# Weight conversion without a clamp and half of its low parts on TensorE, V laid out with zeros, two small copies on ScalarE, one attention layout for all units

## The chip, the cores and the metric

The kernel runs on one core of a Trainium2 chip. The time is device time in microseconds (us) of one execution, and the number compared is the median over several executions. The engines are named as the profile names them: PE (TensorE, the matrix engine; PEld is its weight load), DVE (VectorE), ACT (ScalarE), POOL (GpSimd), SP (SyncE, which here only issues DMAs).

## What is computed

A gated linear attention, a dense layer with a three-way maximum, and a mixture of experts with two of eight experts for each token. All arrays are float32, and the weights of the dense layer reach the chip as 64-bit floats, so that the kernel itself has to make 32-bit numbers of them.

```python
for t in range(S):                                  # B=4, H=8, S=768, D=48
    state = alpha[:, :, t, :, None] * state + np.einsum('bhd,bhe->bhde', k[:, :, t], v[:, :, t])
    y[:, :, t] = np.einsum('bhd,bhde->bhe', q[:, :, t], state)
x = y.transpose(0, 2, 1, 3).reshape(3072, 384)
h = np.maximum(np.maximum(x @ w1, x @ w2), x @ w3)  # 384 -> 768
x = h @ w_out                                       # 768 -> 384
noisy = x @ w_gate + np.log1p(np.exp(x @ w_noise)) * noise
# the two largest of eight, their softmax, then for each chosen expert e:
out[mask] += weight * (np.maximum(x[mask] @ w1[e], 0) @ w2[e])
```

## The kernel before

**Precision by two parts.** The large products are made of fp32r numbers in a high part (`hi`, a cast) and a low part (`lo`, the value minus `hi`), three matmuls for one (`THREE`). So every operand is split on its way: by ACT (the cast) and by DVE or POOL (the subtraction).

**Weights.** Twelve pieces of 128 x 768 64-bit numbers come by DMA into `RAWH`, `RAW` and `RAWO`: nine for the dense layer (`wconv(0)` to `wconv(8)`) and three for the output projection. `dissect` (L200) makes one piece into fp32 with integer operations on the two 32-bit words, in a tile `cb` of which there are two: ACT takes the absolute value of the high word (L206), POOL clamps it from below (L207), DVE shifts it (L208) and puts in the sign and the low bits (L209, L210), ACT casts the high part out (L212) and POOL subtracts to get the low part (L213). A piece can start when one of the two `cb` tiles is free again.

**Attention.** 24 units of 128 rows (two half batches of channels side by side on the partitions), each of four heads' chunks: `prep_a` makes the running product of alpha (`D`, L279) and its reverse (`kh`, L282, and POOL's product with k at L283), and copies eight columns twice on DVE (into `Z` at L277, into `en` at L285). `prep_x` multiplies q (`X1`, `X2`). `prep_v` copies V from the loaded tile `vn` into `vbd`, which holds zeros where one head meets the other (L315); `prep_l` copies V into `l` (L307). On PE: `att_t` transposes `kh`, `att_s` makes the scores, `att_g` the states, `att_y_mm` the output `psY`. Units 0 to 3 (`j < EARLY`) go by another layout than the later ones: q is multiplied by one DVE instruction of 128 partitions instead of two of 64 (L294 instead of L296 and L297), the mask likewise (L340 instead of L344), and `psY` is made of matmuls with 128 x 128 weights (L397) instead of pairs with 64 columns (L402, L403).

**Dense layer, projection, gates.** `ffn(d, f, half)` is 27 matmuls (L451, `p`) into three banks, then one ACT copy (L454), two maxima on DVE (L456) and the split of `H` (L458, L459). The first block of tokens (`d = 0`) is done in halves of 256 tokens, `f0.0.0` to `f0.5.0` first, which needs attention units 0 and 1. `proj` is L466. `gates_t` multiplies the gate weights into the projection's: it adds the two parts of `WO` on POOL (`wf`, L249) and transposes them on PE (L252).

**Order.** The words of `ORDER` call the functions in turn (`w` is a weight piece; `a`, `x`, `v`, `t`, `s`, `g`, `y` the steps of a unit; `f` and `p` dense layer and projection; `i`, `j` gates). In this part the tile scheduler then places each instruction on its engine's queue by its own timeline, so a changed instruction moves others. Each engine and SP's DMA queue works strictly in that order. The experts follow (from L675), in an order written out by hand; the change doesn't touch them, apart from one tile less in each of two rotations (`A`, `C` in `route_h`, L595).

Of the kernel before, what the change touches and what calls it, by code (L numbers as in the profile page):

```python
# [29 lines left out]
EARLY = 4  # L30
# [38 lines left out]
def gla_moe_kernel(ctx: ExitStack, tc: tile.TileContext, qka, qk2, vn, ws, wo, wgn, noise, e1, e2, out):  # L69
# [86 lines left out]
    for z in Z:  # L156
# [43 lines left out]
    def dissect(raw, hi, lo):  # L200
# [12 lines left out]
        nc.gpsimd.tensor_sub(lo, f, hi.bitcast(F32))  # L213
# [5 lines left out]
    def wconv(i):  # L219
# [13 lines left out]
        dissect(raw, d[:, 0], d[:, 1])  # L233
# [37 lines left out]
    def prep_a(j):  # L271
# [5 lines left out]
        nc.vector.tensor_copy(Z[0][:, 0:512:64], a0)  # L277
# [23 lines left out]
    def prep_l(j):  # L301
# [603 lines left out]
```

## Time and profile before

| | us |
|---|---|
| median of 3 runs (lowest, highest) | 977.22 (976.18, 977.25) |
| the profiled execution: its own time | 974.94 |
| the profiled execution: its span, first to last instruction | 973.30 |

| busy in the span | PE | DVE | ACT | POOL |
|---|---|---|---|---|
| us | 912.3 | 496.4 | 400.3 | 310.4 |
| share | 94% | 51% | 41% | 32% |

The program has three stages: up to about 80 us it converts weights and runs the first attention units; from there to about 475 us attention, dense layer and projection go side by side; then come the experts. The page's mean over the span hides that the engines' shares differ between these stages. A busy time of PE counts pipelined matmuls, so full is not the same as at its peak; the granted clock beside it tells which of TensorE's two levels, 1.2 and 2.4 GHz, a stretch had (0.50 to 1.00). Where an engine is idle, the profile names what it waited for.

### The profile page before, as it was taken

The numbers are of one execution on the slowest core, as the hardware profiler recorded it, in microseconds if no ns is written. First come the engines' busy times: TensorE is split into PE (matmuls) and PEld (weight loads), VectorE is DVE, ScalarE is ACT, GpSimd is POOL, SyncE is SP. The second block draws the span as 40 slices with busy tenths as digits, with TensorE's granted clock in tenths as the row PEclk, the third lists the DMA queues.
The fourth block names the chain that finished last, engine by engine and source line by source line (L and its number), as shares of the span: only waits on it lengthen the run. The fifth ranks groups of instructions, "written<-read, shape, count | busy, mean of one in ns | idle before, by whom it ended". The sixth has DMA issues, their size and how long they took to land.

```text
span 973.3 us, 16241 instructions
## 1 busy us (share of the span) xinstructions
PE 912.3 (94%) x6431; PEld 832.5 (86%) x6432; DVE 496.4 (51%) x1006; ACT 400.3 (41%) x806; POOL 310.4 (32%) x293
## 2 busy tenths in 40 slices
PE   4488999999999999999899999999999999999994
PEld 4387899788888778887798999999999999999993
DVE  8998974845877766346654233332333322333110
ACT  5565564543554555332624233332333332333220
POOL 6767640211221211113035333323333333321112
PEclk9669999999999999999999999999999999999997
DMA  9443343323244320221534444443454434422122
GB/s 318 117 139 82 92 82 114 77 57 107 61 106 130 70 63 25 71 62 35 184 101 85 111 110 101 108 96 60 110 115 106 103 54 105 106 58 25 21 25 29
DMA packets 38334, 88.11 MB, mean 91 GB/s; under 512 B 8624, under 2 KB 27312, under 8 KB 38256
## 3 DMA queue, kind: packets, MB, share of 16 engines
q1 hardware_dynamic: 27248, 66.39, 23.9%
q0 software_dynamic: 11008, 20.67, 12.6%
q8 instruction: 51, 0.84, 0.4%
q14 instruction: 27, 0.22, 0.1%
HBM read 64.52 MB, written 20.16 MB: 87 GB/s over the span
## 4 chain that ended last, share of the span: by engine, by line
PE 79%; DVE 8%; DMA 4%; ACT 3%; issue 2%; POOL 2%; SPq 0%; POOLq 0%; DVEq 0%; ACTq 0%
PE psd L761 22%; PE psu L747 22%; PE p L451 21%; PE psl L466 6%; DMA out_dram<-y,idx 2%; PE psx L728 2%; PE psY L402 2%; PE psS L337 1%; POOL cb L207 1%; DMA qka<-in_qka_dram 1%; PE psG L361 1%; DVE D L279 1%; DVE cb L210 1%; PE psT L329 1%; ACT l L307 1%
## 5 line engine op out<-in xcount | busy, mean ns | idle before, releaser
L451 PE MATMUL p<-xt,W 128*128 128x512 f32 (+1 forms) x1188 | 245.2, 360 | 4.6 <-DVE m L456 4.5
L747 PE MATMUL psu<-xe,ew 128*128 128x448 f32 (+1 forms) x1152 | 242.1, 358 | 1.4 <-ACT xe L730 1.4
L761 PE MATMUL psd<-ew,he 128*128 128x384 f32 (+1 forms) x1344 | 242.0, 335 | 0.0
L761 PEld LDWEIGHTS psd<-ew,he 128*128 128x128 f32 (+1 forms) x1344 | 227.0, 180 | 7.9
L451 PEld LDWEIGHTS p<-xt,W 128*128 128x128 f32 x1188 | 195.9, 192 | 36.4 <-DVE m L456 4.9
L747 PEld LDWEIGHTS psu<-xe,ew 128*128 128x128 f32 x1152 | 207.9, 189 | 10.9 <-ACT xe L730 1.5
L751 DVE SCALAR_TENSOR_TENSOR he<-psu,he 128x448 fp32r<-128x448 f32 (+1 forms) x128 | 75.2, 590 | 264.0 <-ACT he L750 264.0
L766 POOL DMA_INDIRECT out_dram<-y,idx x56 | 88.0, 1572 | 150.3 <-ACT y L764 137.4
L764 ACT ACTIVATE y<-psd,GS 128x384 f32<-128x384 f32 (+1 forms) x56 | 32.6, 581 | 205.5 <-PE psd L761 190.7
L750 ACT ACTIVATE he<-psu 128x448 fp32r<-128x448 f32 (+1 forms) x128 | 66.2, 519 | 113.1 <-PE psu L747 113.1
L713 POOL DMA_INDIRECT xg<-x2d,idx x56 | 58.9, 1052 | 73.0 <-DVE r_z L637 33.3
L456 DVE TENSOR_TENSOR m<-p,m 128x512 f32<-128x512 f32 (+1 forms) x88 | 51.7, 589 | 48.3 <-PE p L451 41.4
L459 POOL TENSOR_TENSOR H<-m,H 128x512 fp32r<-128x512 f32 (+1 forms) x34 | 41.0, 1209 | 110.0 <-ACT H L458 109.9
L694 DVE TENSOR_TENSOR ew<-raw,ew 128x768 fp32r<-128x768 f32 x64 | 57.8, 962 | 31.6 <-ACT ew L693 30.9
L466 PE MATMUL psl<-WO,H 128*128 128x400 f32 x336 | 68.3, 348 | 0.0
L283 POOL TENSOR_TENSOR kh<-qka,kh 128x512 f32<-128x512 f32 x24 | 33.3, 1388 | 105.5 <-DVE kh L282 37.0
L466 PEld LDWEIGHTS psl<-WO,H 128*128 128x128 f32 x336 | 60.1, 188 | 1.6 <-issue 0.5
L732 POOL COPY GS<-xg 128x1 f32<-128x1 f32 (+1 forms) x56 | 11.1, 236 | 129.8 <-DMA xg<-x2d,idx 129.8
L693 ACT CAST ew<-raw 128x768 fp32r<-128x768 f32 x64 | 48.8, 832 | 2.8 <-DMA raw<-in_e_dram 2.8
L458 ACT CAST H<-m 128x512 fp32r<-128x512 f32 (+1 forms) x34 | 18.5, 544 | 52.6 <-DVE m L456 52.5
L344 DVE TENSOR_TENSOR x<-psS,mask 64x512 f32<-64x512 f32 x40 | 27.4, 686 | 23.0 <-PE psS L338 22.5
L337 PEld LDWEIGHTS psS<-x,kh 64*64 64x64 f32 x384 | 27.2, 146 | 13.9 <-DVE x L294 7.7
(158 smaller groups left out, 1114.6 us busy)
## 6 DMA issues: line engine op xcount, KB each, us to landing
raw<-in_e_dram SPq DMA_DIRECT2D x32, 768.0 KB, 5.1
qka<-in_qka_dram SPq DMA_DIRECT2D x44, 289.7 KB, 4.5
RAW<-in_ws_dram SPq DMA_DIRECT2D x7, 768.0 KB, 4.8
out_dram<-z SPq DMA_DIRECT2D x5, 960.0 KB, 4.5
vn<-in_vn_dram SPq DMA_DIRECT2D x24, 192.0 KB, 2.7
x2d<-x2t SPq DMA_DIRECT2D x24, 192.0 KB, 1.9
RAWO<-in_wo_dram SPq DMA_DIRECT2D x3, 768.0 KB, 4.4
xt<-sg SPq DMA_DIRECT2D x72, 32.0 KB, 2.8
```

The source lines that it names most:

```text
L451: nc.tensor.matmul(ps, W[:, f, w, a, k], x[:, k, b], start=n == 0, stop=n == 8)
L456: nc.vector.tensor_max(m, ps, m)
L459: nc.gpsimd.tensor_sub(lo, m, hi.bitcast(F32))
L466: nc.tensor.matmul(ps, place(d, f)[:, a, 128 * t:128 * t + 128], WOT[0][:, b, f], start=n == 0, stop=n == 17)
L693: nc.scalar.copy(hi, r)
L694: nc.vector.tensor_sub(EW[e, m][:, 1, s], r, hi.bitcast(F32))
L713: nc.gpsimd.indirect_dma_start(out=XG[n, i][0:w], out_offset=None, in_=x2d if h else x2d[0:128 + LATE], in_offset=bass.IndirectOffsetOnAxi ...
L747: nc.tensor.matmul(ps, w[:, a, f, k], XE[n][:, k, b], start=i == 0, stop=i == 8)
L750: nc.scalar.activation(hi, ps, AF.Relu)
L751: nc.vector.scalar_tensor_tensor(HE[n][:, f, 1], ps, 0.0, hi.bitcast(F32), op0=OP.max, op1=OP.subtract)
L761: nc.tensor.matmul(ps, HE[n][:, f, a, o:o + m], w[:, b, f], start=j == 0, stop=j == 23)
L766: nc.gpsimd.indirect_dma_start(out=out, out_offset=bass.IndirectOffsetOnAxis(ap=IDX[h][0:m, 1, c:c + 1], axis=0), in_=y, in_offset=None, c ...
```

## The change

- `dissect` drops the clamp: ACT scales the high word by a power of two (still one instruction), and DVE's shift follows directly; POOL's L207 is gone for all twelve pieces. For pieces 0 to 5 the low part is no longer POOL's subtraction: PE multiplies the value with the identity in fp32 and adds the high part times minus the identity in fp32r, in two halves of 384 columns, and ACT copies each half out of PSUM.
- V comes from memory with its zeros, twice as long (128 x 768), into two tiles `vbd0`, `vbd1`; the copies of `prep_v` (L315) and the zeroing of `vbd` are gone. The load of the unit after next is issued after `att_g` instead of after `prep_l`.
- Units 0 to 3 use the layout of the later ones; `l` becomes `la`, `lb` for two parities.
- The two copies of eight columns (L277, L285) go from DVE to ACT.
- `gates_t` transposes both parts of `WO` with matmuls against minus the identity and accumulates them; POOL's addition is gone.
- The one-hot tiles `A`, `C` of the routing have five buffers instead of six.

```diff
+PELOW = 6
...
+    minus = const.tile([128, 128], FR, name="minus")
...
-    VN = [at.tile([128, 2, 2, 2, 48], F32, name=f"vn{i}") for i in range(2)]
-    L = [at.tile([128, 2, 4, 128], F32, name=f"l{i}") for i in range(2)]
-    VBD = at.tile([128, 2, 2, 2, 2, 48], F32, name="vbd")
+    VBD = [at.tile([128, 2, 2, 2, 2, 48], F32, name=f"vbd{i}") for i in range(2)]
+    LA = [at.tile([128, 2, 4, 64], F32, name=f"la{i}") for i in range(2)]
+    LB = [at.tile([128, 2, 4, 64], F32, name=f"lb{i}") for i in range(2)]
...
+    nc.scalar.activation(minus, ident, AF.Copy, scale=-1.0)
...
-        nc.scalar.activation(b, high.bitcast(F32), AF.Abs)
-        nc.gpsimd.tensor_scalar(b, b, TINY, None, op0=OP.max)
-        nc.vector.tensor_scalar(a, a, 5, 2, op0=OP.logical_shift_left, op1=OP.logical_shift_right)
-        nc.vector.scalar_tensor_tensor(a, high, 0xC0000000, a, op0=OP.bitwise_and, op1=OP.bitwise_or)
+        nc.scalar.activation(b, high.bitcast(F32), AF.Copy, scale=2.0 ** -112)
+        nc.vector.tensor_scalar(a, a, 3, None, op0=OP.logical_shift_left)
+        nc.vector.scalar_tensor_tensor(a, high, 0x80000000, a, op0=OP.bitwise_and, op1=OP.bitwise_or)
         nc.vector.scalar_tensor_tensor(a, low, 29, a, op0=OP.logical_shift_right, op1=OP.bitwise_or)
         f = b.rearrange("p (a d) -> p a d", a=2)
         nc.scalar.copy(hi, f)
-        nc.gpsimd.tensor_sub(lo, f, hi.bitcast(F32))
+        if i >= PELOW:
+            nc.gpsimd.tensor_sub(lo, f, hi.bitcast(F32))
+            return
+        for h in range(2):
+            ps = pl.tile([128, 400], F32, tag="l2", name="pslo")[:, 0:DM]
+            nc.tensor.matmul(ps, ident, f[:, h], start=True, stop=False)
+            nc.tensor.matmul(ps, minus, hi[:, h], start=False, stop=True)
+            nc.scalar.copy(lo[:, h], ps)
...
-        wf = cv.tile([128, DM], F32, tag="cb", name="wf", bufs=2)
-        nc.gpsimd.tensor_add(wf, WOT[0][:, 0, f, 0:DM].bitcast(F32), WOT[0][:, 1, f, 0:DM].bitcast(F32))
...
-            nc.tensor.transpose(pt[:, 128 * k:128 * k + 128], wf[:, 128 * k:128 * k + 128], ident)
+            for a in range(2):
+                nc.tensor.matmul(pt[:, 128 * k:128 * k + 128], WOT[0][:, a, f, 128 * k:128 * k + 128], minus,
+                                 start=a == 0, stop=a == 1)
...
-        nc.vector.tensor_copy(Z[0][:, 0:512:64], a0)
+        nc.scalar.copy(Z[0][:, 0:512:64], a0)
...
-        nc.vector.tensor_copy(EN[j].rearrange("p a b -> p (a b)"), D[:, 63:512:64])
+        nc.scalar.copy(EN[j].rearrange("p a b -> p (a b)"), D[:, 63:512:64])
...
-        if j < EARLY:
-            nc.vector.tensor_mul(X1[j], t[:, 0:512], D)
-        else:
-            nc.vector.tensor_mul(X1[j][64:128], t[64:128, 0:512], D[64:128])
-            nc.vector.tensor_mul(X2[j][0:64], t[0:64, 0:512], D[0:64])
+        nc.vector.tensor_mul(X1[j][64:128], t[64:128, 0:512], D[64:128])
+        nc.vector.tensor_mul(X2[j][0:64], t[0:64, 0:512], D[0:64])
...
-        for par in range(2):
-            o = 64 * par
-            nc.scalar.copy(VBD[o:o + 64, :, :, :, par, :].rearrange("q h p a e -> q (h p a) e"),
-                           VN[i][o:o + 64].rearrange("q h p a e -> q (h p a) e"))
-        if j > EARLY:
-            prep_l(j)
+        prep_l(j)
...
+        if j + 2 < 24:
+            load_v(j + 2)
...
-                A = small([128, 128], "A", F16, 6)
-                C = small([128, 192], "C", F16, 6)
+                A = small([128, 128], "A", F16, 5)
+                C = small([128, 192], "C", F16, 5)
```

Lines below the changed ones have other numbers in the changed kernel: L205 to L207 there are DVE's three steps of `dissect` (L208 to L210 before), L204, L209 and L217 ACT's scaling, cast and copy of a low half, L215 and L216 the two new matmuls, L433 is the dense layer's matmul.

How the order moves is shown at three places. The first is PE's queue where the dense layer begins (`p`); `psY` is the output of a unit (`x_269`, `x_270` belong to unit 2, `x_385`, `x_386` to unit 3). Before:

```order
L397 MATMUL psY<-x_270,l_102 128x64
L397 MATMUL psY<-x_269,l_103 128x64
L451 MATMUL p<-xt_112,W 128x256 x18
L397 MATMUL psY<-x_386,l_102 128x64
L397 MATMUL psY<-x_385,l_103 128x64
```

After (`x_281`, `x_282` belong to unit 2, `x_415`, `x_416` to unit 3, and `pslo` is the low part of a weight piece):

```order
L350 MATMUL psG<-vbd_102,kt 64x48x2
L433 MATMUL p<-xt_114,W 128x256 x18
L215 MATMUL pslo<-cb,ident 128x384 x2
L216 MATMUL pslo<-W,minus 128x384 x2
L433 MATMUL p<-xt_114,W 128x256 x9
L384 MATMUL psY<-x_415,la_104 64x64
L385 MATMUL psY<-x_416,lb_106 64x64
L433 MATMUL p<-xt_114,W 128x256 x18
L384 MATMUL psY<-x_281,la_103 64x64
```

The dense layer stood behind all of unit 2's output; it now begins ahead of nearly all of it, and one weight piece's low part stands behind its first 18 matmuls.

The second place is DVE's queue where a weight piece and unit 3's `prep_a` meet. Before:

```order
L277 COPY Z_105<-qka_99 128x8
L209 SCALAR_TENSOR_TENSOR cb<-RAW,cb 128x768
L375 SCALAR_TENSOR_TENSOR st<-psG,ae 128x480
L279 SCALAR_TENSOR_TENSOR D<-qka_99,Z_105 128x512
L210 SCALAR_TENSOR_TENSOR cb<-RAW,cb 128x768
L280 RECIPROCAL Z_106<-D 128x8
L285 COPY en<-D 128x8
L208 TENSOR_SCALAR cb<-cb 128x768
L277 COPY Z_105<-qka_98 128x8
L282 SCALAR_TENSOR_TENSOR kh<-qka_99,Z_106 128x512
```

After:

```order
L286 SCALAR_TENSOR_TENSOR kh<-qka_99,Z_108 128x512
L205 TENSOR_SCALAR cb<-cb 128x768
L283 SCALAR_TENSOR_TENSOR D<-qka_100,Z_107 128x512
L206 SCALAR_TENSOR_TENSOR cb<-RAW,cb 128x768
L284 RECIPROCAL Z_108<-D 128x8
L297 TENSOR_TENSOR x_415<-qka_100,D 64x512
L298 TENSOR_TENSOR x_416<-qka_100,D 64x512
L403 TENSOR_TENSOR xt_114<-psY,xt_114 128x256
L207 SCALAR_TENSOR_TENSOR cb<-RAW,cb 128x768
L286 SCALAR_TENSOR_TENSOR kh<-qka_100,Z_108 128x512
```

The two copies are gone from the queue, and q's product has become two instructions.

The third place is ACT's queue around the weight pieces 2 and 3. Before:

```order
L315 COPY vbd<-vn_100 64x8x48 x2
L331 COPY kt<-psT 128x512
L378 COPY l_103<-st 64x8x48
L379 COPY l_103<-st 64x8x48
L354 COPY ae<-en 128x96x4
L212 CAST W<-cb 128x2x384
L206 ACTIVATE cb<-RAW 128x768
```

After:

```order
L395 CAST xt_114<-psY 128x2x256
L217 CAST W<-pslo 128x384 x3
L209 CAST W<-cb 128x2x384
L204 ACTIVATE cb<-RAW 128x768
L367 COPY la_104<-st 64x8x48
L368 COPY lb_106<-st 64x8x48
L217 CAST W<-pslo 128x384
L281 COPY Z_107<-qka_99 128x8
```

The copies into `vbd` are replaced by the copies of low halves, and the `Z` copy, on which unit 2's `D` on DVE now waits, stands between them.

## Rows read from the trace of the kernel before

**Rows 1.** Stretches: us, busy us of PE, PEld, DVE, ACT, POOL (instructions), PEclk, DMA share, GB/s.

```profile
0.00:80.00 80.00, 44.57 (x398) 41.13 (x400) 73.49 (x92) 47.40 (x90) 56.28 (x46) 0.78 0.59 181
20.00:60.00 40.00, 19.71 (x180) 17.66 (x179) 37.31 (x46) 21.11 (x37) 30.09 (x14) 0.63 0.56 156
80.00:100.00 20.00, 20.00 (x205) 18.91 (x205) 17.49 (x29) 9.59 (x20) 14.22 (x12) 0.95 0.31 77
100.00:475.00 375.00, 369.02 (x3144) 316.52 (x3144) 245.72 (x581) 182.42 (x394) 86.63 (x75) 1.00 0.31 80
```

**Rows 2.** Waits of PE up to 90 us: us in total, times, longest.

```profile
PE psT L329 <- POOL kh L283: 14.5, 3, 8.5
PE psS L337 <- DVE x L294: 7.4, 1, 7.4
```

**Rows 3.** Groups of DVE up to 88 us: busy us, mean ns | idle before, releaser.

```profile
L209 DVE SCALAR_TENSOR_TENSOR cb<-RAW,cb 128x768 uint32<-128x768 uint32 x7 | 12.0, 1716 | 0.1
L208 DVE TENSOR_SCALAR cb<-cb 128x768 uint32<-128x768 uint32 x10 | 11.3, 1131 | 3.0 <-POOL cb L207 2.8
...
L210 DVE SCALAR_TENSOR_TENSOR cb<-RAW,cb 128x768 uint32<-128x768 uint32 x7 | 7.6, 1091 | 0.1
...
L285 DVE COPY en<-D 128x8 f32<-128x8 f32 x7 | 3.9, 559 | 0.0
L277 DVE COPY Z<-qka 128x8 f32<-128x8 f32 x8 | 3.8, 478 | 1.0 <-DMA qka<-in_qk_dram 0.8
L210 DVE SCALAR_TENSOR_TENSOR cb<-RAWH,cb 128x768 uint32<-128x768 uint32 x2 | 3.4, 1698 | 0.0
```

**Rows 4.** Timeline, 34 to 37 us: start, us, engine, line, instruction.

```profile
34.09 0.93 DVE L210 SCALAR_TENSOR_TENSOR cb<-RAW,cb 128x768 uint32<-128x768 uint32 x1
...
35.05 0.12 DVE L285 COPY en<-D 128x8 f32<-128x8 f32 x1
35.08 0.55 DVE L208 TENSOR_SCALAR cb<-cb 128x768 uint32<-128x768 uint32 x1
...
36.11 2.32 POOL L213 TENSOR_TENSOR W<-cb,W 128x768 fp32r<-128x768 f32 x1 [3.72 <-ACT W L212]
36.76 2.49 DVE L209 SCALAR_TENSOR_TENSOR cb<-RAW,cb 128x768 uint32<-128x768 uint32 x1
```

**Rows 5.** Groups of POOL up to 88 us.

```profile
L207 POOL TENSOR_SCALAR cb<-cb 128x768 f32<-128x768 f32 x10 | 25.6, 2563 | 4.1 <-ACT cb L206 4.0
L213 POOL TENSOR_TENSOR W<-cb,W 128x768 fp32r<-128x768 f32 x9 | 19.0, 2109 | 11.7 <-ACT W L212 11.7
L283 POOL TENSOR_TENSOR kh<-qka,kh 128x512 f32<-128x512 f32 x6 | 9.4, 1559 | 7.0 <-DVE kh L282 5.2 <-PE p L451 1.8
```

**Rows 6.** Groups over the span (of L315 up to 88 us).

```profile
L344 DVE TENSOR_TENSOR x<-psS,mask 64x512 f32<-64x512 f32 x40 | 27.4, 686 | 23.0 <-PE psS L338 22.5
...
L315 ACT COPY vbd<-vn 64x384 f32<-64x384 f32 x10 | 5.1, 505 | 0.1
...
L475 ACT COPY x2t<-psl 128x384 f32<-128x384 f32 x24 | 11.6, 487 | 0.0
...
L474 ACT COPY nl<-psl 128x16 f32<-128x16 f32 x24 | 4.2, 174 | 34.3 <-PE psl L466 34.3
...
L252 PE MATMUL pst<-ident,wf 128*128 128x128 f32 x18 | 3.2, 275 | 0.0
```

**Rows 7.** Timeline of PE at five places.

```profile
34.94 3.56 PE L397 MATMUL psY<-x,l 128*128 128x64 f32 x30 [0.50 <-ACT l L379]
...
93.23 3.49 PE L451 MATMUL p<-xt,W 128*128 128x256 f32 x27
...
101.60 0.27 PE L402 MATMUL psY<-x,l 128*64 128x64 f32 x1
...
102.58 0.26 PE L363 MATMUL psG<-vbd,kt 128*64 128x96 f32 x1
...
103.50 4.57 PE L451 MATMUL p<-xt,W 128*128 128x256 f32 x36
```

More of the change, by code (lines that the diff above doesn't have):

```diff
@@ L29 @@
 NBK = 24
-EARLY = 4
 HEAD = 384
@@ L165, in gla_moe_kernel @@
                                 base=0, channel_multiplier=-1)
-    nc.vector.memset(VBD, 0.0)
     nc.gpsimd.memset(AE, 0.0)
     for i in range(2):
-        nc.gpsimd.memset(L[i], 0.0)
+        nc.gpsimd.memset(LA[i][64:128], 0.0)
+        nc.gpsimd.memset(LA[i][0:64, :, :, 48:64], 0.0)
+        nc.gpsimd.memset(LB[i][0:64], 0.0)
+        nc.gpsimd.memset(LB[i][64:128, :, :, 48:64], 0.0)
     def late_consts():
@@ L232, in wconv @@
             d = WOT[0][:, :, f:f + 2, 0:DM]
-        dissect(raw, d[:, 0], d[:, 1])
+        dissect(i, raw, d[:, 0], d[:, 1])
         for k in NEXT.get(i, ()):
@@ L301, in prep_l @@
     def prep_l(j):
-        i = 0 if j < EARLY else j % 2
+        i = j % 2
         for par in range(2):
@@ L306, in prep_l @@
                 d = X[i][64 * ab:64 * ab + 64].rearrange("q p (h par) e -> q par h p e", par=2)
-                nc.scalar.copy(d[:, par, :, :, 0:48], VN[j % 2][o:o + 64, :, :, ab, :])
-        if j + 2 < 24:
-            load_v(j + 2)
+                nc.scalar.copy(d[:, par, :, :, 0:48], VBD[j % 2][o:o + 64, :, :, ab, par, :])
     def prep_v(j):
-        i = j % 2
-        for par in range(2):
-            o = 64 * par
-            nc.scalar.copy(VBD[o:o + 64, :, :, :, par, :].rearrange("q h p a e -> q (h p a) e"),
-                           VN[i][o:o + 64].rearrange("q h p a e -> q (h p a) e"))
-        if j > EARLY:
-            prep_l(j)
+        prep_l(j)
     def bank(j, name, early=False):
@@ L337, in att_s @@
             nc.tensor.matmul(ps[0:64, s], KH[j][64:128, s], X1[j][64:128, s], start=True, stop=True)
-            nc.tensor.matmul(ps[64:128, s], KH[j][0:64, s], (X1 if j < EARLY else X2)[j][0:64, s], start=True, stop=True)
-        if j < EARLY:
-            nc.vector.tensor_mul(X2[j].rearrange("p (c t) -> p c t", c=8), ps.rearrange("p (c t) -> p c t", c=8),
-                                 mask[:, None, :].to_broadcast([128, 8, 64]))
-            return
+            nc.tensor.matmul(ps[64:128, s], KH[j][0:64, s], X2[j][0:64, s], start=True, stop=True)
         for X, o in ((X1, 0), (X2, 64)):
@@ L390, in att_y_mm @@
         ps = YP[j] = pa.tile([128, 2, 256], F32, tag="a", name="psY")
-        for p in range(2 if j < EARLY else 0):
-            for c in range(4):
-                sc = slice(64 * c, 64 * c + 64)
-                sx = slice(256 * p + 64 * c, 256 * p + 64 * c + 64)
-                for k, X in enumerate((X2, X1)):
-                    nc.tensor.matmul(ps[:, p, sc], L[k][:, p, c], X[j][:, sx], start=k == 0, stop=k == 1)
-        for p in range(2 if j >= EARLY else 0):
+        for p in range(2):
             for c in range(4):
@@ L864, in layout @@
     qk2[:, :, 0:48] = qka[0:2]
-    vn = v.reshape(4, 2, 2, 2, 3, 2, 128, 48).transpose(0, 4, 1, 6, 5, 2, 3, 7).reshape(24, 128, 384)
+    vt = v.reshape(4, 2, 2, 2, 3, 2, 2, 64, 48).transpose(0, 4, 1, 6, 7, 5, 2, 3, 8)
+    vn = np.zeros((4, 3, 2, 2, 64, 2, 2, 2, 2, 48), v.dtype)
+    for par in range(2):
+        vn[:, :, :, par, :, :, :, :, par] = vt[:, :, :, par]
+    vn = vn.reshape(24, 128, 768)
     rows = []
```

17 lines of the change are left out of this document (6 added, 11 removed).

## The prediction

> **What bounds the kernel now.** I read the table of stretches first. Over the first 80 us PE is busy 44.57 us and so stands idle 35.4, while DVE is busy 73.49; from 100 to 475 us PE is busy 369.02 of 375 [rows 1]. What the change can win therefore lies before 80 us: later, PE waits 6 us in all, and the experts behind are not touched. Then PE's waits: the two longest are for POOL's `kh` (14.5 us) and DVE's product with q (7.4 us) [rows 2]. POOL's `kh` itself waits for DVE's scan, 5.2 of its 7.0 us of idle time [rows 5]. So both end at DVE's queue: DVE is the engine that has no gap, and when it gets through its list is when PE becomes full.
>
> Last, why DVE is full. Its groups have means far above what one instruction takes undisturbed: at 34 to 35.6 us a logical step L210 takes 0.93 us, a shift L208 0.55, a copy of eight columns 0.12; at 36.76 us a logical step L209 of the same shape takes 2.49, and ends only after POOL's subtraction (36.11 to 38.43) has [rows 4]. Against these bare times the groups up to 88 us hold an excess of: L209 12.0 - 7 x 0.93 = 5.5; L208 11.3 - 10 x 0.55 = 5.8; L210 7.6 - 6.5 = 1.1 and 3.4 - 1.9 = 1.5; L285 3.9 - 7 x 0.12 = 3.1; L277 3.8 - 8 x 0.12 = 2.8 [rows 3, 4]. Together **19.8 us** of DVE's time is standing behind POOL.
>
> **The change part by part**, in DVE's time up to 88 us, since that sets when PE is full.
>
> *POOL's part of the conversion.* In that time POOL works 25.6 us on the clamp, 19.0 on nine low parts and 9.4 on `kh` [rows 5], 54.0 in all. The clamp goes, and six of nine low parts; 9.4 + 3/9 x 19.0 = 15.7 stay, 29%. If the excess goes with POOL's work, 0.71 x 19.8 = **-14.1 us**. Bounds: -19.8, if what stays seldom meets DVE; about -7, if DVE meets the remaining work as often as it met twice as much. I take -14.1, since the one collision shown is with a subtraction, of which some stay. The wait of DVE's shift for the clamp goes too: **-2.8** [rows 3].
>
> *Copies to ACT.* The 15 bare copies leave DVE: 15 x 0.12 = **-1.8** (their excess is counted above).
>
> The Trainium skill (SBUF — State Buffer, section "Who interferes with whom") states that DVE and GpSimd hold a shared port pair as an exclusive lock for a whole instruction, and that ScalarE never waits on anyone. The trace agrees as far as [rows 4] goes. By that rule the excess of the two copies, 5.9 us, goes whole once they are on ACT, not to 71%: the sum would be 1.7 us better.
>
> *One layout for all units.* For units 0 to 3 the product with q and the mask become two instructions each of 64 partitions, and such an instruction costs 0.686 us [rows 6] at half the partitions, because the columns are the same. Eight more: 8 x 0.69 = **+5.5**. On PE the layout gives time back: a `psY` of the old kind is 32 records of 3.56/30 = 0.119 us, 3.8 us; of the new kind it takes 101.60 to 102.58, 0.98 us [rows 7]; four units, -11.3 us at the full clock.
>
> *Low parts on PE.* Twelve fp32 and twelve fp32r products of 384 columns. An fp32r one costs at most 1.5 x 3.49/27 = 0.19 us, from the 256-column ones. For fp32, `psG`'s eight pairs of records of 96 columns take 102.58 to 103.50, 0.115 a pair, two records to a product, so 0.23 us; four times the columns make at most 0.92, and twice the fp32r price, 0.38, is the least [rows 7]. That is 6.8 to 13.3 us at the full clock, about what `psY` gives back, and it falls where PE is idle 20.3 of 40 us [rows 1]. I cost it at **0**; if that cover is gone it is a rival below.
>
> The Trainium skill (FP8 and Floating Point Precision, section "TensorE Precision Notes") gives true fp32 four passes. By the page, as an estimate, a product of 384 columns is 4 x 160 ns = 0.64 us, between my ends; PE's extra would be about 10 us, and the sum stays.
>
> *ACT.* It gains 12 copies of 0.487 us (5.8) and 15 of about 0.174 (2.6), and loses the ten `vbd` copies, 5.1 [rows 6]: +3.3 net on 47.40 of 80 us [rows 1]. Its load is no bound, but its order is: DVE's scan `D` now waits for the `Z` copy, which stands in ACT's queue behind copies of low halves and the casts that wait for DVE, and behind it wait the scalings of the next pieces. Nothing of before shows that wait. The least is 0, the most is that DVE waits for ACT's whole new work, 8.4 us. I take a third of the net, **+1.0**, as the queue has 32 us of gaps.
>
> *Gates.* 18 transposes (3.2 us busy [rows 6]) become 36 matmuls of 128 columns, in a time when PE is full. A 256-column one takes 0.13 [rows 7], so 36 cost between 2.3 (half of it) and 4.7: -0.9 to +1.5, I take **+0.5**. POOL's additions were not late there.
>
> *At no cost.* V with zeros doubles 24 transfers. Two of them stand ahead of the weights: 2 x 128 x 384 x 4 bytes more at 181 GB/s, the mean of the first 80 us [rows 1], are at most 2.2 us, in which DVE has the first two units to do; later the DMA engines are 31% busy. Its issue now waits for PE's `psG` in SP's queue, and behind it stand the next loads of q, k, alpha and the weights; they have a unit's time (20 units in 375 us, some 18 us each). `A` and `C` with five buffers: the second pair of a group waits one product sooner; DVE makes them while PE is in long products.
>
> **Sum:** -14.1 - 2.8 - 1.8 + 5.5 + 1.0 + 0.5 = **-11.7 us**. Against the profiled execution's own 974.94 us this is 963.2; the median of the runs stands 2.3 above that execution, so **965.5 us**. What is late next is PE itself: dense-layer matmuls stand ahead of unit 2's output in its new order, so PE has work as soon as unit 1's `psY` and the first two pieces are there. The gain isn't given back afterwards, since the stage from 100 us has only 6 us of idle time, and DVE has less to do there, not more.
>
> **The rivals.**
>
> *All of the excess goes.* DVE seldom meets POOL any more. For: the remaining POOL work is at single places. Against: `kh` must be made where DVE is busiest. -19.8 in place of -14.1: 959.8; with ACT's and the gates' terms at their least (-1.0 and -1.4), 957.4.
>
> *The clock and PE's new work bound the start.* From 20 to 60 us the granted clock was 0.63 on the mean [rows 1], nearer the lower of the two levels. At that level the twelve pairs cost up to 26.6 us, less 11.3 for two units' `psY`: 15.3. If the stage shrinks by 11.7, its idle time shrinks from 20.3 to 8.6, and 6.7 don't fit. Then PE, not DVE, sets when the dense layer is under way: 972.2. Against: this takes the dearest price for fp32, and where PE had work without a gap, from 80 us, the clock was 0.95.
>
> *Slower: the `cb` ring closes through PE.* A piece's tile now becomes free only when PE has read it, and PE is in order: one low part stands behind 18 dense matmuls, 2.3 us at the full clock and 4.7 at half. While it waits, ACT's next scaling waits, and behind that ACT's copies out of PSUM and the `Z` copy, so DVE stops too. If each of the six pieces costs such a wait of more than 12.7/6 = 2.1 us (the gain without ACT's term), the change loses; at 3.2 us each, +6.5: 983.7. For: only two `cb` tiles. Against: five of six stand behind short work.
>
> *It doesn't move the end.* The start is shorter, but a later unit of attention is late by as much, since its loads are issued by units now closer together: 977. Against: PE's 6 us.
>
> **How the numbers follow.** Forecast 0.53, all of the excess 0.15, the clock 0.15, the end not moved 0.06, the ring 0.11. Faster by over 0.2% (2 us, about what a measurement can tell from no change) are the first three: 0.83; the same 0.06; slower 0.11. The range goes from 957 to 974: it takes in the first three and leaves out the others, 0.17.
>
> **What would show it.** Right: L205 to L207 of the changed kernel near 0.55, 0.93, 0.93 us on the mean except beside `kh` and three subtractions; PE's wait for POOL's `kh` shorter by several us; PE full (20.00 of 20) from about 68 us in place of 80; the stage from 100 us with no more than some 6 us of idle PE. Wrong: DVE idle behind ACT's `Z` copy or scaling for more than a few us, ACT's scaling waiting for PE, PE busy but at the lower level beyond 70 us, or a stretch on DVE that stays although POOL is idle.

## The result, and the profile after

The changed kernel takes **965.74 us** (median; 964.74 to 966.60), the kernel before 976.72 beside it: ratio 0.9887, 95% interval 0.987 to 0.9904, so some 11 us faster (9.4 to 12.7). The forecast of 965.5 stands. Its own profiled execution took 966.48 us, with a span of 964.8.

Three views of the changed kernel. The stretches, with the columns of [rows 1]:

```profile
0.00:80.00 80.00, 58.30 (x560) 47.09 (x562) 72.22 (x100) 52.56 (x115) 28.71 (x41) 0.87 0.67 200
20.00:60.00 40.00, 33.11 (x312) 25.15 (x313) 35.84 (x50) 29.03 (x62) 8.14 (x5) 0.83 0.70 188
80.00:100.00 20.00, 16.67 (x194) 15.69 (x196) 17.57 (x25) 9.27 (x21) 8.16 (x6) 1.00 0.48 149
100.00:475.00 375.00, 368.10 (x3093) 317.83 (x3089) 236.21 (x541) 170.18 (x392) 74.44 (x66) 1.00 0.33 88
```

PE's longest waits up to 90 us, as [rows 2], then the longest of DVE and ACT up to 80 us:

```profile
PE psT L322 <- POOL kh L287: 10.5, 2, 8.5
PE p L433 <- DVE m L438: 4.1, 1, 4.1
PE pslo L215 <- ACT W L217: 3.3, 2, 1.9
```

```profile
DVE D L283 <- ACT Z L281: 3.0, 3, 1.8
DVE cb L205 <- ACT cb L204: 1.5, 1, 1.5
ACT Z L281 <- DMA qka<-in_qka_dram: 7.8, 3, 3.7
```

And the groups of DVE and POOL up to 88 us, as [rows 3, 5]. L205 is the shift, L206 and L207 the two logical steps, L211 the low parts that stayed on POOL:

```profile
L286 DVE TENSOR_TENSOR_SCAN kh<-qka,Z 128x512 f32<-128x512 f32 x7 | 10.8, 1538 | 0.2
L207 DVE SCALAR_TENSOR_TENSOR cb<-RAW,cb 128x768 uint32<-128x768 uint32 x7 | 8.0, 1148 | 0.0
L206 DVE SCALAR_TENSOR_TENSOR cb<-RAW,cb 128x768 uint32<-128x768 uint32 x7 | 6.6, 946 | 0.1
L205 DVE TENSOR_SCALAR cb<-cb 128x768 uint32<-128x768 uint32 x11 | 6.5, 594 | 3.4 <-ACT cb L204 3.4
L298 DVE TENSOR_TENSOR x<-qka,D 64x512 f32<-64x512 f32 x6 | 6.0, 1006 | 0.1
...
L287 POOL TENSOR_TENSOR kh<-qka,kh 128x512 f32<-128x512 f32 x7 | 12.1, 1735 | 39.7 <-DVE kh L286 34.6 <-DMA qka<-in_qka_dram 3.7 <-PE p L433 1.3
...
L211 POOL TENSOR_TENSOR W<-cb,W 128x768 fp32r<-128x768 f32 x3 | 5.5, 1844 | 8.3 <-ACT W L209 8.3
```

PE's idle time before 80 us falls from 35.4 to 21.7, POOL's busy time is halved, and the shift and the first logical step stand at 0.594 and 0.946 where they stood at 1.131 and 1.716 [rows 3]. From 100 us on PE is idle for 6.9 us, before 6.0. That the time is won in the first stage and kept shows at a fixed point of the program, the last 36 products of the dense part's projection, on PE's timeline of before (first line) and after (second):

```profile
472.08 6.77 PE L466 MATMUL psl<-WO,H 128*128 128x400 f32 x36
```

```profile
464.65 6.77 PE L448 MATMUL psl<-WO,H 128*128 128x400 f32 x36
```

They start 7.4 us earlier, and the span ends 8.5 earlier: the experts give 1.1.

**Two sums** serve the experiments below. The first is DVE's *excess*: for each instruction of DVE's timeline that starts before 80 us, its time less the short time that its form and shape take in these kernels, summed, and put down to the POOL instruction that it lay beside longest. The second is PE's account up to the end of those 36 products: idle time; time lost to the clock (busy time of 5 or 10 us stretches times one less the granted clock); and the rest, PE's work at the full clock. The column "gain" is the ratio of medians made into us at a before of 976.7; the other columns are of one profiled execution each. Executions of one kernel differ in their clock: the mean granted clock over the span is 0.962 to 0.974 in those of the kernel before, and the profiled one has 0.973. So a few us in the column of the clock need not belong to the kernel.

| kernel | gain, us | excess | beside clamp | beside subtractions | beside `kh` |
|---|---|---|---|---|---|
| before | 0 | 20.9 | 5.0 | 11.7 | 3.2 |
| no clamp alone | 2.3 | 17.4 | - | 12.2 | 3.8 |
| after | 11.0 | 7.9 | - | 3.6 | 2.8 |
| all low parts on POOL | 3.0 | 14.1 | - | 10.7 | 2.7 |
| discarded subtractions | 6.7 | 14.9 | - | 7.7 + 3.0 | 3.5 |
| discarded maxima | 11.5 | 9.3 | 1.8 (maxima) | 2.0 | 4.1 |
| all of W's low parts on PE | 15.5 | 4.9 | - | 1.4 | 1.8 |
| discarded products | 9.6 | 13.6 | - | 7.2 | 3.9 |

| kernel | end of the 36 | idle | lost to the clock | work |
|---|---|---|---|---|
| before | 478.9 | 41.4 | 10.6 | 426.9 |
| after | 471.4 | 31.9 | 9.6 | 429.9 |
| one layout alone | 482.8 | 47.4 | 16.3 | 419.1 |
| all low parts on POOL | 480.2 | 52.7 | 9.5 | 417.9 |
| discarded products | 472.5 | 35.9 | 5.3 | 431.4 |
| before, with discarded products | 483.4 | 33.0 | 10.2 | 440.3 |
| all of W's low parts on PE | 465.1 | 25.2 | 5.6 | 434.3 |

### The profile page after: what moved, and what is told of

It reads as the page before. It is cut to its first block, busy times and chain, and to the rows that moved or that the text cites. A ratio compares the mean times of both kernels' runs of the same rounds, so it can differ in the third digit from the quotient of the medians.

```text
span 964.8 us, 16310 instructions
## 1 busy us (share of the span) xinstructions
PE 914.0 (95%) x6485; PEld 828.6 (86%) x6486; DVE 480.8 (50%) x965; ACT 387.4 (40%) x819; POOL 264.9 (27%) x275
## 3 DMA queue, kind: packets, MB, share of 16 engines
q0 software_dynamic: 11008, 20.67, 12.2%
## 4 chain that ended last, share of the span: by engine, by line
PE 81%; DVE 7%; DMA 4%; ACT 3%; issue 2%; POOL 1%; SPq 0%; POOLq 0%; DVEq 0%; ACTq 0%
PE psd L743 23%; PE psu L729 23%; PE p L433 20%; PE psl L448 6%; DMA qka<-in_qka_dram 2%; PE psx L710 2%; PE psY L384 2%; DMA out_dram<-y,idx 1%; PE psS L330 1%; PE psG L348 1%; DVE D L283 1%; DVE cb L207 1%; DVE kh L286 1%; DVE x L298 1%; PE psT L322 1%
## 5 line engine op out<-in xcount | busy, mean ns | idle before, releaser
L433 PE MATMUL p<-xt,W 128*128 128x512 f32 (+1 forms) x1188 | 244.3, 361 | 6.2 <-DVE m L438 4.1
L433 PEld LDWEIGHTS p<-xt,W 128*128 128x128 f32 x1188 | 196.6, 193 | 38.1 <-DVE m L438 4.4
L333 DVE TENSOR_TENSOR x<-psS,mask 64x512 f32<-64x512 f32 x48 | 32.9, 686 | 21.5 <-PE psS L331 21.2
L713 DVE TENSOR_TENSOR xe<-psx,xe 128x384 fp32r<-128x384 f32 (+1 forms) x56 | 28.9, 520 | 15.1 <-ACT xe L712 15.1
```

The lines of the kernel that those rows point to most:

```text
L433: nc.tensor.matmul(ps, W[:, f, w, a, k], x[:, k, b], start=n == 0, stop=n == 8)
```

## Experiments: one part of the change alone

**The clamp alone** (the kernel before, converting without it).

```diff
-        nc.scalar.activation(b, high.bitcast(F32), AF.Abs)
-        nc.gpsimd.tensor_scalar(b, b, TINY, None, op0=OP.max)
+        nc.scalar.activation(b, high.bitcast(F32), AF.Copy, scale=2.0 ** -112)
...
```

(The shift and the first logical step have the changed kernel's constants, too.)

> The kernel before with one part of the change alone: the conversion scales on ScalarE, and POOL's clamp is gone; POOL keeps all nine low parts. Theory of the prediction (DVE is stretched in proportion to POOL's work beside it): POOL's work up to 88 us falls from 54.0 to 28.4 us, so 0.47 x 19.8 = 9.4 us of DVE's excess goes, and the 2.8 us of wait for the clamp: about 12 us faster, 964.5 us, with the mean of the shift near 0.8 us instead of 1.13. Rival A (the subtractions of the low parts stretch DVE, as in the one collision shown; the clamp seldom does): only the wait and little more goes, 972 to 974 us. Rival B (not DVE's time but the chain through POOL held the start: scaling, clamp, shift): also faster, by up to 2.6 us for each of the pieces on the chain, but with the means of DVE's steps unchanged.

Measured: 975.52 us, ratio 0.9976 (0.9966 to 0.9986). 25.6 us of POOL's work bought 2.3 us. Its groups of DVE and POOL up to 88 us:

```profile
L209 DVE SCALAR_TENSOR_TENSOR cb<-RAW,cb 128x768 uint32<-128x768 uint32 x7 | 11.0, 1576 | 0.1
...
L208 DVE SCALAR_TENSOR_TENSOR cb<-RAW,cb 128x768 uint32<-128x768 uint32 x7 | 8.2, 1172 | 0.1
L207 DVE TENSOR_SCALAR cb<-cb 128x768 uint32<-128x768 uint32 x12 | 8.0, 664 | 2.0 <-ACT cb L206 2.0
...
L276 DVE COPY Z<-qka 128x8 f32<-128x8 f32 x8 | 2.7, 342 | 4.1 <-DMA qka<-in_qka_dram 3.1 <-DMA qka<-in_qk_dram 0.9
...
L212 POOL TENSOR_TENSOR W<-cb,W 128x768 fp32r<-128x768 f32 x9 | 19.4, 2153 | 24.4 <-ACT W L211 24.4
```

The shift (here L207) came down to 0.664 as the theory said, and the first logical step (here L208) from 1.716 to 1.172, but the second (here L209) rose from 1.091 to 1.576, so the two together hardly moved (19.2 us, before 19.6): the excess fell by 3.5 us, not 9.4, and the 2.8 us of wait for the clamp came back as waits for ACT and for the load of q, k and alpha. Rival A, that the subtractions do the stretching, fits better than the prediction's rule, though less was won than its 972 to 974 us.

The order moved too. The last step of the nine dense-layer pieces on DVE, before (first line) and without the clamp (second):

```profile
76.31 0.96 DVE L210 SCALAR_TENSOR_TENSOR cb<-RAW,cb 128x768 uint32<-128x768 uint32 x1
```

```profile
59.59 2.48 DVE L209 SCALAR_TENSOR_TENSOR cb<-RAW,cb 128x768 uint32<-128x768 uint32 x1
```

DVE had these pieces done 15 us earlier, and 2.3 us came of it: the sixth and seventh scans of `kh` end later (at 74.5 in place of 71.9, and 95.4 in place of 91.6), and PE, busy 9.35 us from 70 to 80, had a granted clock of 0.50 there. So the 2.3 us are the clamp together with another order.

**One layout alone** (the kernel before with `EARLY = 0`).

> The kernel before with the second layout for all units, the first four too; nothing else changed. Prediction's term: eight more instructions of 64 partitions on DVE, 8 x 0.69 = +5.5 us, so 982.2 us. Rival A (PE's shorter output products, 11.3 us less in the first four units, matter in the start too): 977 us or less. Rival B (the new instructions of DVE are stretched as the others are, by 1.3 to 1.8): +7 to +10, 984 to 987 us.

Measured: 980.34 us, ratio 1.0032 (1.002 to 1.0045), +3.1 us, between the term of 5.5 and rival A's nothing. PE's work is 7.8 us less there, and 6.0 of idle time and 5.7 of clock take its place. The clock's share is that of one execution: it has 0.965 on the mean, and the other nine of this kernel 0.972 to 0.977. The order moved here as well: the last of the nine dense-layer pieces is done on DVE at 93.6 us in place of 77.3.

**Low parts all on POOL** (the changed kernel with `PELOW = 0`).

> The changed kernel with all nine low parts on POOL, none on PE. Theory of the prediction: six subtractions come back to POOL (12.7 us, 28.4 of 54 us in all), so DVE's excess is 10.4 instead of 5.7 us, +4.7, less 12 copies on ScalarE that were off the path: about 970 us. Rival A (PE's fp32 products and ScalarE's copies out of PSUM cost as much in PE's or ScalarE's queue as POOL's collisions do): 964 to 967 us, the same as the changed kernel. Rival B (the ring of two conversion tiles closes through PE): faster than the changed kernel by over 2 us, below 963.5 us.

Measured: 975.15 us, ratio 0.9969 (0.996 to 0.9979): 8.0 us slower than the changed kernel, where 4.7 was expected. Rivals A and B fall, and the low parts on PE are the greatest part of the change. DVE is back at its old pace:

```profile
L206 DVE SCALAR_TENSOR_TENSOR cb<-RAW,cb 128x768 uint32<-128x768 uint32 x7 | 11.8, 1679 | 0.0
```

**The small copies back on DVE** (the changed kernel, otherwise).

```diff
-        nc.scalar.copy(Z[0][:, 0:512:64], a0)
+        nc.vector.tensor_copy(Z[0][:, 0:512:64], a0)
...
-        nc.scalar.copy(EN[j].rearrange("p a b -> p (a b)"), D[:, 63:512:64])
+        nc.vector.tensor_copy(EN[j].rearrange("p a b -> p (a b)"), D[:, 63:512:64])
```

> The changed kernel with the copies of eight columns (starts and ends of the decay) back on DVE. Theory of the prediction: DVE gets 15 x 0.12 = 1.8 us and some excess (up to 1.7) back, and loses 1.0 us of waiting for ScalarE: 966.5 to 968.5 us. Rival (ScalarE's queue stands still for 6.3 us behind a copy that waits for the load of q, k and alpha, and with it the scalings and the copies of low parts behind; DVE waits for ScalarE some 5 us in all): 2 to 5 us faster than the changed kernel, 961 to 964 us, and DVE's waits for ScalarE fall from about 5 to under 3 us.

Measured: 969.80 us, ratio 0.9917 (0.9901 to 0.9934): 2.9 us slower than the changed kernel, with intervals that just touch. The rival, a gain, falls. Its DVE waited for the load itself:

```profile
DVE Z L281 <- DMA qka<-in_qka_dram: 4.5, 4, 1.6
DVE Z L281 <- DMA qka<-in_qk_dram: 1.7, 1, 1.7
```

So the 3.0 us that the changed kernel's scan waits for ACT's copy are mostly not ACT's queue: the data isn't there earlier.

**The old gates** (the changed kernel with POOL's addition and 18 transposes).

> The changed kernel with the old gates: POOL adds the two parts of W's second matrix and TensorE transposes the sum, 18 transposes in place of 36 products. Prediction's term: new gates cost +0.5 (-0.9 to +1.5), so 964.3 to 966.6 us here, taken 965.2. Rival (POOL's additions have two operands in SBUF and stretch DVE as the subtractions do, six of some 1.8 us at 70 to 110 us, where DVE is still busy nearly the whole time): 967 to 970 us.

Measured: 965.59 us, ratio 0.9884 (0.9868 to 0.9899), the same as the changed kernel. The new gates cost nothing that can be measured, as the theory said, and POOL's additions at that place did no harm.

**Half of V** (the changed kernel; `load_v` fetches 384 of 768 columns).

> The changed kernel that loads only the first half of each V tile, as many bytes as before the change; the other half of V is left out and stays zero. Theory of the prediction (the doubled transfers cost nothing): 964 to 967 us, and ScalarE's copy still waits for the load of q, k and alpha some 7 us in all before 80 us. Rival (the doubled transfers hold up the loads of q, k and alpha in the queues): ScalarE's wait falls to under 3 us and the time by 2 to 4 us, 961.5 to 964 us.

This kernel leaves out half of V, and POOL clears that half of both tiles once at the start. Measured: 967.51 us, ratio 0.9901 (0.9884 to 0.9917): not faster. After the first units ACT waits as long as before for q, k and alpha (7.8 us in both kernels), so the zeros in V's transfers do not cause that wait. For the first units it waits longer (3.5 us, 0.6 in the changed kernel), and DVE's first scan starts 1.3 us later, so a gain of that size could be hidden here, but not the 2 to 4 us of the rival:

```profile
ACT Z L284 <- DMA qka<-in_qka_dram: 7.8, 3, 4.1
```

## Experiments: which work of POOL stretches DVE

The changed kernel, with six instructions on POOL whose result nobody reads: first the same subtraction, then a maximum in the clamp's form, which takes POOL longer.

```diff
+        nc.gpsimd.tensor_sub(XW2[1][:, 0, :, 0:384], f, hi.bitcast(F32))
```

```diff
+        if i < PELOW:
+            nc.gpsimd.tensor_scalar(XW2[1][:, 0, :, 0:384], f, 0.5, None, op0=OP.max)
```

> The changed kernel, whose six pieces with low parts on TensorE now also make POOL do the same subtraction into a tile that nobody reads: POOL's work beside DVE is back, but nobody waits for its result. The result is discarded work only. Theory (a subtraction on POOL, with two operands in SBUF, stands in the way of DVE's instructions): DVE's excess before 80 us rises by six times some 1.2 us, +7 us, and the time to 971 to 974 us, near the kernel with all low parts on POOL (975.15). Rival (the start was held by the chain through POOL to the low part that PE waits for, not by DVE's stretched steps): no more than +2 us, 965 to 968 us.

> The same six pieces, but POOL's discarded instruction is a maximum against a constant over the same 768 elements, the clamp's form, with one operand in SBUF; it takes POOL some 2.5 us, longer than the subtraction's 2.1. Theory of the prediction (DVE's excess goes with POOL's busy time, whatever the instruction): 0.37 us of excess for each us of POOL, 6 x 2.5 x 0.37 = +5.5 us, 970 to 972 us, as much as with the subtractions. Rival, from the kernel without the clamp, where only 3.5 us of DVE's excess went with 25.6 us of POOL's work (0.14 us for each us): 6 x 2.5 x 0.14 = +2 us of excess, 966 to 968 us.

Measured: 969.91 us, ratio 0.9931 (0.9915 to 0.9948), with the subtractions, 4.3 us slower than the changed kernel and between what theory and rival had said; 964.40 us, ratio 0.9882 (0.9859 to 0.9906), with the maxima, no slower. The groups on POOL (first the subtractions, then the maxima):

```profile
L218 POOL TENSOR_TENSOR xt<-cb,W 128x768 fp32r<-128x768 f32 x6 | 12.7, 2112 | 15.1 <-ACT W L209 9.4 <-DMA qka<-in_qka_dram 5.7
```

```profile
L210 POOL TENSOR_SCALAR xt<-cb 128x768 fp32r<-128x768 f32 x6 | 15.3, 2542 | 17.4 <-DVE cb L207 13.2 <-DMA RAW<-in_ws_dram 4.3
```

12.7 us of subtractions made 7.0 us more of excess, 15.3 us of maxima 1.4. It can be read off single instructions. With the subtractions (POOL's and DVE's timeline), a logical step that starts beside one takes 2.45 us and ends at 23.42, 0.82 us after the subtraction:

```profile
20.40 2.20 POOL L218 TENSOR_TENSOR xt<-cb,W 128x768 fp32r<-128x768 f32 x1 [5.80 <-ACT W L209]
...
20.97 2.45 DVE L207 SCALAR_TENSOR_TENSOR cb<-RAWH,cb 128x768 uint32<-128x768 uint32 x1
```

With the maxima, one runs beside a maximum and takes its bare 0.96, and the next loses half a microsecond:

```profile
18.21 2.37 POOL L210 TENSOR_SCALAR xt<-cb 128x768 fp32r<-128x768 f32 x1 [3.66 <-DVE cb L207]
22.03 2.30 POOL L210 TENSOR_SCALAR xt<-cb 128x768 fp32r<-128x768 f32 x1 [1.44 <-DVE cb L207]
...
19.92 0.96 DVE L206 SCALAR_TENSOR_TENSOR cb<-RAWH,cb 128x768 uint32<-128x768 uint32 x1
...
22.38 1.46 DVE L206 SCALAR_TENSOR_TENSOR cb<-RAW,cb 128x768 uint32<-128x768 uint32 x1
```

The kernel before says the same: its clamp ran from 29.97 to 32.40, and a logical step in the midst of it took 0.94:

```profile
29.97 2.43 POOL L207 TENSOR_SCALAR cb<-cb 128x768 f32<-128x768 f32 x1
...
31.04 0.94 DVE L209 SCALAR_TENSOR_TENSOR cb<-RAW,cb 128x768 uint32<-128x768 uint32 x1
```

Counted over all of them, each of the six subtractions held up one of DVE's instructions, by 0.5 to 1.6 us, and each of the six maxima by 0.6 us at most. DVE's instruction need not have two operands for that: beside a subtraction of the kernel before (43.17 to 44.96) a shift, which has one, took four times its bare 0.55:

```profile
43.23 2.15 DVE L208 TENSOR_SCALAR cb<-cb 128x768 uint32<-128x768 uint32 x1 [2.02 <-POOL cb L207]
```

So POOL's two forms differ, and the prediction's rule, excess in proportion to POOL's busy time, is refuted. That POOL's result was late is no part of it either: nobody reads these subtractions, and they still cost 4.3 us. (They do keep a `cb` tile longer: ACT's scaling waits 2.3 us for them. How much of the 4.3 that is was not tried.)

## Experiments: what TensorE's new work does

**All of W's low parts on PE** (`PELOW = 9`).

> The changed kernel with all nine low parts of W on TensorE. Theory (each subtraction on POOL costs DVE some 1.2 us, PE has room): three fewer, DVE's excess before 80 us from 7.9 to about 4.3, 962 to 963.5 us. Rival (PE is already full when the last three pieces come, from 60 us on; their six fp32 and six fp32r products of some 0.65 us cost PE 3 to 7 us): 966 to 970 us.

Measured: 960.91 us, ratio 0.9841 (0.9824 to 0.9859): 4.5 us faster than the changed kernel, a little more than the theory said. Both logical steps are bare on the mean:

```profile
L206 DVE SCALAR_TENSOR_TENSOR cb<-RAW,cb 128x768 uint32<-128x768 uint32 x7 | 6.6, 945 | 0.1
L207 DVE SCALAR_TENSOR_TENSOR cb<-RAW,cb 128x768 uint32<-128x768 uint32 x7 | 6.6, 942 | 0.0
```

**The products without their use.** POOL makes all nine low parts, and PE does the 24 products of the first six pieces anyway.

```diff
+        nc.gpsimd.tensor_sub(lo, f, hi.bitcast(F32))
         if i >= PELOW:
-            nc.gpsimd.tensor_sub(lo, f, hi.bitcast(F32))
             return
...
-            nc.scalar.copy(lo[:, h], ps)
```

> As the kernel with all low parts on POOL (975.15), but TensorE also does the 24 products of the six pieces, and nobody reads them: discarded work only. It has DVE's whole excess (about 14 us before 80 us, as the kernels with 14.2 and 14.9 us) and the chain through POOL, but TensorE is kept at work early. Theory A (the 5 us between the kernel with discarded subtractions, 969.9, and the one with all low parts on POOL, 975.15, are TensorE's granted clock, 0.85 against 0.63 from 20 to 60 us): the clock rises to 0.8 or more and the time falls to 970 to 972 us. Theory B (they are the way to the dense layer, which there waits for POOL's low part): the clock rises, but the time stays at 974 to 977 us.

Measured: 967.35 us, ratio 0.9902 (0.9887 to 0.9918). By adding 13.5 us of useless work to PE this kernel became 6.6 us faster than the one with all low parts on POOL, at the same excess on DVE (13.6 and 14.1). Theory B falls, and theory A had said 970 to 972. The stretch from 20 to 60 us, without (first line) and with the products:

```profile
20.00:60.00 40.00, 14.84 (x188) 12.37 (x188) 38.50 (x42) 20.40 (x43) 21.05 (x9) 0.63 0.72 186
```

```profile
20.00:60.00 40.00, 26.25 (x273) 19.06 (x273) 39.15 (x45) 21.81 (x45) 20.82 (x9) 0.89 0.73 190
```

The clock rose from 0.63 to 0.89. But DVE's order differs too: without the products the scan of unit 2's state stands behind a logical step that met a subtraction, with them ahead of it. Its row on DVE's timeline, first without, then with:

```profile
54.78 2.15 DVE L206 SCALAR_TENSOR_TENSOR cb<-RAW,cb 128x768 uint32<-128x768 uint32 x1
56.85 1.15 DVE L364 TENSOR_TENSOR_SCAN st<-psG,ae 128x480 f32<-128x480 f32 x1
```

```profile
52.18 1.15 DVE L363 TENSOR_TENSOR_SCAN st<-psG,ae 128x480 f32<-128x480 f32 x1
53.24 1.20 DVE L285 TENSOR_TENSOR_SCAN kh<-qka,Z 128x512 f32<-128x512 f32 x1
54.36 2.51 DVE L206 SCALAR_TENSOR_TENSOR cb<-RAW,cb 128x768 uint32<-128x768 uint32 x1
```

And behind that scan PE stood: without the products it waited 18.1 us in four pieces for ACT's copy `la` of the state, with them 1.9.

```profile
PE psY L384 <- ACT la L367: 18.1, 4, 7.8
```

This run also bounds what the subtractions alone cost. It has all of them on POOL, and the changed kernel, which has ACT's copies of the low halves besides, is only 1.4 us faster (the intervals overlap) with 5.7 us less excess. So excess on DVE isn't time one for one: taking the subtractions away, with the products on PE kept, was worth 1.4 us by this run and 4.3 by the discarded ones, and most of the 8.0 us of the low parts can be had without it.

**The same products in the kernel before**, with all of POOL's and DVE's work.

```diff
...
         nc.gpsimd.tensor_sub(lo, f, hi.bitcast(F32))
+        if i >= 6:
+            return
+        for h in range(2):
+            ps = pl.tile([128, 400], F32, tag="l2", name="pslo")[:, 0:DM]
+            nc.tensor.matmul(ps, ident, f[:, h], start=True, stop=False)
+            nc.tensor.matmul(ps, hi[:, h, 0:128], hi[:, h], start=False, stop=True)
```

> The kernel before, with nothing of the change but the 24 products of the first six pieces on TensorE, whose results nobody reads (the second of each pair with weights out of the high part itself, since there is no room for another tile): discarded work only. All of POOL's and DVE's work stays. Theory A (most of what the low parts on TensorE gave, 7.8 us of 9.4, was TensorE being kept at work early: a higher granted clock, and so shorter ways through it): the mean clock from 20 to 60 us rises from 0.63 to 0.8 or more, and the time falls by 4 to 8 us, 968.5 to 973 us. Theory B (the 7.8 us were the other order that the scheduler found, a state's scan 4.7 us earlier on DVE, and not the clock): the clock rises, but the time stays within 2 us of 976.5, or rises by the products themselves, up to 6 us.

Measured: 981.26 us beside 980.23, ratio 1.0017 (0.9996 to 1.0037): no gain, as theory B had it, though the clock rose as in the other pair:

```profile
20.00:60.00 40.00, 34.23 (x256) 27.46 (x255) 35.06 (x46) 23.53 (x45) 22.95 (x12) 0.83 0.58 158
```

Theory A, that the clock is what the low parts on PE gave, is not general then: here PE's time lost to the clock stayed at 10.2 us, since there was more work to do at the lower level, and 13.4 us of new work went where PE was idle or made PE later. What of the 6.6 us of the other pair was clock (4.2 us less is lost to it) and what the order found by the scheduler is **not settled**; no kernel here has the one without the other.

## An experiment for the load

The changed kernel with `PELOW = 9` and the load of alpha split from that of q and k, so that it is issued when the second scan is done.

```diff
...
+        if j + 2 < 24:
+            load(j + 2, ((1024, 1545),))
         nc.gpsimd.tensor_mul(R, t[:, 512:1024], R)
...
-            load(j + 2)
+            load(j + 2, ((0, 1024),))
```

> The changed kernel with all nine low parts of W on TensorE (960.9 alone), and with the load of a unit's decay split from that of its q and k, so that it is issued once DVE's second scan has read the tile, not once POOL has made kh and DVE the products with q. Theory (ScalarE's copy of the starts waits some 8 us before 80 us for this load, and DVE's first scan some 3 us for the copy): ScalarE's wait falls to under 4 us, DVE's under 1.5, and the time to 957.5 to 960 us. Rival (DVE has other work while it waits, or twice the number of transfers holds up the queue): 960 to 963 us, no gain.

Measured: 959.56 us, ratio 0.9818 (0.9804 to 0.9831), the fastest of all; beside `PELOW = 9` alone the ratio is 0.0023 lower, with intervals that overlap (0.9824 to 0.9859), so some 2 us, not told apart for sure. ACT's wait for the load is gone from its list of waits before 80 us, where it was 8.4 us with `PELOW = 9` alone, and DVE's wait for ACT's copy is 2.0 in place of 3.1. The wait was real. Whether it was cheap because DVE had other work, as the rival had it, is not shown.

## Why the prediction was right, point by point

**What bounds the kernel.** Right as to the place: the gain lies before 80 us, where DVE is the busiest engine. That DVE's list sets when PE is full, us for us, is not borne out: with the clamp alone gone DVE was done with the dense-layer pieces 15 us earlier for 2.3 us, and with the discarded products 6.6 us were won at the same excess. PE's longest wait is still for `kh` (8.5 us, the first unit, which no part of the change touches).

**POOL's part of the conversion, -14.1.** As a sum of excess it was right, its division wrong, and its price in time too high. DVE's excess before 80 us fell from 20.9 to 7.9, by 13.0. But the prediction gave the clamp 25.6/54 of it, 9.4 us, and the six subtractions 4.7. Alone, the clamp took 3.5 us of excess and 2.3 us of time with it; putting the subtractions back costs 6.2 to 7.0 us of excess and 4.3 to 8.0 us of time. The step that failed is "if the excess goes with POOL's work": it goes above all with POOL's work that has two operands in SBUF. With its wait of 2.8, the clamp was priced at 12.2 us and was worth 2.3 alone; the low parts were priced at 4.7 and were worth 8.0. The one collision shown in [rows 4] was with a subtraction; I noted it and still divided by busy time. In the excess the errors cancelled because the change takes away most of both. That the time came out as well is in good part luck: the clamp's price was too high, and what the products on PE gave was not in the sum.

By the Trainium skill (SBUF — State Buffer, section "Who interferes with whom") a DVE instruction with two inputs in SBUF contends with any GpSimd instruction that reads SBUF. The trace agrees where a subtraction ran beside a logical step (2.45 us in place of 0.96). It agrees less where a maximum with one operand did, which reads SBUF too: there one step took 0.96 and the next 1.46, and the measurement decides.

**The wait for the clamp, -2.8, and ACT, +1.0.** The wait went, but DVE's waits for ACT before 80 us are 4.5 us (3.0 for `Z`, 1.5 for the scaling), not 1.0. For `Z` the cause is mostly not the one named, ACT's order, but the load: with the copies on DVE it waits 6.2 us for the load itself.

**Copies, -1.8.** With their excess they are worth more: put back, they take 5.0 us of DVE's time before 80 us (3.0 and 2.0), and the kernel is 2.9 us slower.

**One layout, +5.5.** +3.1 alone. The price on DVE was as told for the mask (0.683 each, L333); the products with q took more (0.844 and 1.006, L297 and L298), stretched as other instructions are. PE's shorter `psY` (7.8 us less work) may give part of it back already in the start, where the prediction counted none; with the order moved as well, +3.1 is not split further.

**Low parts on PE, 0.** Right as to cover: PE's work up to the fixed point is 429.9 us before the clock, 3.0 more than before, and its idle time fell by 9.5. The price lay between the ends: at the full clock (granted 1.00) four records, two products of 384 columns in fp32, take 1.45 us, and two fp32r ones 0.52 (of the kernel with `PELOW = 9`):

```profile
55.93 1.45 PE L215 MATMUL pslo<-cb,ident 128*128 128x384 f32 x4
...
60.95 0.52 PE L216 MATMUL pslo<-W,minus 128*128 128x384 f32 x2
```

One of the four lasts 0.48 us, so they start 0.32 apart; one of the two lasts 0.34, so they start 0.18 apart. Where another stands behind it, an fp32 product thus costs 0.64 us (0.38 to 0.92 predicted) and an fp32r one 0.18 (at most 0.19 predicted), 9.8 us for six pieces; with the end of the last, which the next overlaps, it is 0.72 and 0.26, 11.8 us. The Trainium skill's four passes (FP8 and Floating Point Precision, "TensorE Precision Notes"), with an estimate of 0.64, agree with it. What the prediction missed is an effect of this work: with the early stretch fuller the granted clock there was 0.83 in place of 0.63. Whether the time came of the clock or of the order stays open, as said above; that it came with the products, and not only with the lighter POOL, the discarded products show.

**Gates, +0.5, and V's zeros, 0.** Right within what can be measured (0.3; and half of V is no faster).

**The rivals.** The ring of `cb` tiles did not close through PE: ACT's scaling has no wait for PE before 80 us (one of 1.9 us in the kernel with the copies on DVE), and more pieces on PE made the kernel faster. The clock did not bind PE at the start: the stretch with the most new work had the higher clock. The end moved. All of the excess did not go, but it nearly can: 4.9 us are left with `PELOW = 9`.

**What would show it.** PE was to be full from about 68 us. It isn't: it is busy 9.21 us from 70 to 80, but 16.67 of 20 from 80 to 100, where before it had been full. These 3.3 us are given back; PE's waits there are for DVE (1.3, 1.2 and 0.7 us). It is in the sum: from profiled execution to profiled execution the gain is 8.5 us, where the steps said 11.7. The medians differ by 11.0, because the profiled execution of before lay 1.8 under its median and that of after 0.7 above it. Some 2 us of the fit of 965.5 to 965.74 are therefore luck, beside the luck in the terms.

**The parts together.** Measured one at a time, they give -2.3 (clamp), +3.1 (layout), -2.9 (copies), -8.0 (low parts) and +0.3 (gates): -9.8 of -11.0. Each was measured with the order that the scheduler found for it, so that the sum comes near is no proof of the single figures.

## What to carry to other kernels

Before moving work off an engine because it "shares a port" with the busy one, sort its instructions by form and look at single pairs on the timeline: here 19 us of subtractions cost DVE more than twice as much as 26 us of a clamp. An idle TensorE is a cheap place for such work even in fp32, at 3.6 times the fp32r price (0.64 and 0.18 us), as long as it stands idle for want of something else. Time that an engine wins isn't time of the kernel until the order lets it be: 15 us earlier on DVE gave 2.3. And a sum that comes out right does not prove its terms: only the parts alone showed which of them carried the gain.

## What the runs showed of the hardware that I had not expected

- A POOL instruction with two SBUF operands cost DVE 0.55 us for each us (7.0 for 12.7), one with a constant as its second operand 0.09 (1.4 for 15.3). DVE's instructions with one operand are held up too (a shift 2.15 us in place of 0.55).
- The stretching goes both ways: POOL's `kh` multiply, 1.26 us at its shortest here, took 3.44 beside DVE's scans and logical steps:

```profile
35.63 3.44 POOL L287 TENSOR_TENSOR kh<-qka,kh 128x512 f32<-128x512 f32 x1 [21.17 <-DVE kh L286]
```

- Discarded products on TensorE raised the granted clock of the early stretch from 0.63 to 0.83 and 0.89, and in one of two kernels the time fell with it.
